# An S4D convolution and a PEER layer on one core: decays by direct exponentials, wider sine tiles, and a new order of the tables

## The chip, the cores and the metric

The kernel runs on one core of one Trainium2 chip. The metric is the device time of one execution in microseconds (us). Three executions of the kernel before took 502.75, 501.16 and 500.92 us, so its median is 501.16 us. The core has five engines with a program of their own each: TensorE (PE, with its weight loads listed as PEld), VectorE (DVE), ScalarE (ACT), GpSimd (POOL) and SyncE (SP), which issues the DMA transfers. Each runs its instructions in order, and they wait for one another by semaphores. SBUF holds 128 partitions; PSUM has eight banks of 512 fp32 words per partition, which TensorE writes and DVE and ACT read.

## The reference

Two layers on a sequence of 2048 tokens with 512 channels. The first is an S4D convolution with 128 complex states for each channel:

```python
dt = jnp.exp(log_dt)
A = -jnp.exp(log_A_real) + 1j * A_imag
C = (C_real + 1j * C_imag) * dt[:, None]
P = jnp.exp((A * dt[:, None])[:, :, None] * pos[None, None, :])
K = 2.0 * jnp.einsum("dn,dnl->dl", C, P).real
y = jnp.fft.irfft(jnp.fft.rfft(u_t, L2) * jnp.fft.rfft(K, L2)[None, :, :], L2)[:, :, :L]
return y.transpose(0, 2, 1) + u * D_skip[None, None, :]
```

It is applied to the layer norm of `x = A_u`, and `h = x + ...`. The second layer picks, for each of 32 heads, the best of 16 x 16 experts by two products with keys, and adds the expert's value times a gelu; its input is the layer norm of `h`.

## The kernel before

The work falls into a front half, the convolution, which ends about 298 us into the span, and a back half, the PEER layer. The change touches the front half alone.

The convolution of length 2048 is done as matmuls with transform matrices, in four **quarters** c of 128 channels. For each quarter there is

- `u_s1` and `k_s1`: stage 1 of the transform of the input (tile s1u) and of the kernel (s1k), four pieces kt for each. A piece is 32 matmul records with 64 columns of weights and 128 columns moved, and two copies of 128x512 by ACT out of PSUM. The input pieces `xs` are normed first, by a subtraction and a product on DVE.
- `u_s2` and `k_s2`: stage 2 (s2yu, s2yk), eight pieces for each. On the s2yk pieces DVE multiplies the two spectra (yk and U). In the last quarter, one of its three products is done on POOL (U from ki, L743), for which ACT copies ki out of PSUM.
- `k_ia`: the first inverse stage (ia), eight pieces, into T, from which ib makes the output later.

The kernel K that s1k takes is made from 32 **tables**, i = 0 to 31, eight for each quarter and 16 channels in each. A table needs the phases and the decays of 128 states at 64 short and 32 long distances, 96 columns for each channel; a state stands on each partition. `phases` (POOL, L557) adds step angles into the tile pg. `powers` (POOL, L570 to L573) builds the decays by repeated products from eleven exponentials per channel, the tile E, which ACT makes at L373; the second half of E goes to DRAM (e_d) and comes back later. `heads` (L579 to L581) multiplies the amplitudes Mg in. `mags` (L588) makes 64 columns of each channel of the tile mg by one outer product of eight heads and eight steps, and `tails` (L594) the other 32, the far distances. Then `trig` on ACT makes the sine (L647) and the cosine (L644 and L645) of the phases into PSUM tiles of one bank each, and six products on DVE (L651 to L664) form gf (sine) and mg (cosine). `kgen` (L690) multiplies each table's far and near columns into kps, and ACT and DVE take K from there.

Steps, bases, powers and heads are made for 64 channels at a time (tiles PS and TS, two buffers each); pg, mg and gf have two buffers each. All PSUM tiles of the front half are of one bank, from a pool psA of seven; psK holds the norm's mean and deviation (pc).

The order of all operations on all engines is a table of numbers, ORDER, in which the operations of the plan are emitted; an engine runs its operations in that order and never another. SP issues all loads, also in that order. The products of w_q with the keys (wps, wh, w_d) for the back half are spread through the front half, and go through DRAM.

## Time and profile before

| what | us |
|---|---|
| median of three executions | 501.16 |
| the profiled execution | 502.31 |
| its span in the profile | 500.5 |
| first s1u matmul | 71.98 |
| first ib matmul | 297.91 |
| busy in the span: PE, DVE, ACT, POOL | 448.6, 408.5, 300.2, 325.0 |

Busy time of an engine is the time in which it has at least one instruction; the chain of a profile is the sequence of work and waits that ended last, followed back from the end. A row of a group names the line, the engine, the operation, the tile written and those read, and the shape with the count; behind the bar stand the busy time in us, the mean of one in ns, and how long the engine was idle just before these instructions, and for what. A row of a stretch gives its start and end and its length in us, the busy time of the engines with the number of instructions, the clock granted to TensorE, the share of the DMA engines and GB/s. A row of the chain in order of time gives the start, the length, and what ran.

### The profile page before, as it was taken

The page shows a single profiled execution, that of the slowest core. Times are in us where ns is not written, and L with a number is a line of the kernel's source. Part 1 is how long each engine was busy: PE and PEld are TensorE (multiplying, and loading weights), DVE is VectorE, ACT ScalarE, POOL GpSimd, SP SyncE. Part 2 cuts the span into 40 slices and gives each one's busy share as a digit, 9 for nine tenths or more (in the row PEclk, how much of TensorE's full clock was granted, in tenths as well). Part 3 has the DMA queues.
Part 4 walks back from the last instruction along what each step waited for, and adds up shares of the span by engine and source line. Part 5 has one row for each costly group of instructions (what it writes and reads, how often), then busy time and mean ns, then how long its engine had stood idle before and what let it go on. Part 6 is the DMA issues. An engine that isn't in the chain of part 4 may idle for free.

```text
span 500.5 us, 16696 instructions
## 1 busy us (share of the span) xinstructions
PE 448.6 (90%) x7206; PEld 393.6 (79%) x7206; DVE 408.5 (82%) x708; ACT 300.2 (60%) x596; POOL 325.0 (65%) x344
## 2 busy tenths in 40 slices
PE   0545879999999999999999689999999999999985
PEld 0324669989999989999998688887878888787874
DVE  4879998989988998799775494878979686978994
ACT  4796789986997689966996263454043430416231
POOL 3988997999999999989864303652263516535130
PEclk9999979999999999999999899999999999999999
DMA  7916885354200740045242757320171311010012
GB/s 259 413 52 211 275 297 173 145 156 195 65 3 9 266 131 24 3 102 218 64 162 72 227 158 251 110 103 1 61 226 54 117 56 44 1 45 0 1 51 78
DMA packets 27361, 61.04 MB, mean 122 GB/s; under 512 B 7028, under 2 KB 14456, under 8 KB 26136
## 3 DMA queue, kind: packets, MB, share of 16 engines
q1 hardware_dynamic: 27288, 59.98, 35.3%
q8 instruction: 56, 0.92, 0.8%
q14 instruction: 17, 0.14, 0.1%
HBM read 46.08 MB, written 13.89 MB: 120 GB/s over the span
## 4 chain that ended last, share of the span: by engine, by line
PE 69%; DVE 19%; ACT 5%; issue 2%; DMA 2%; POOL 1%; SPq 0%; ACTq 0%; DVEq 0%
PE sc L1150 14%; PE ia L764 12%; PE s1k L471 6%; PE kps L690 6%; PE s1u L471 5%; DVE oh L1280 5%; PE s2yu L488 5%; PE xu L1157 4%; PE s2yk L488 3%; PE ib L1036 3%; PE o L1327 2%; PE wps L828 2%; PE cnt L1290 2%; DVE U L733 2%; DMA wq<-wq 2%
## 5 line engine op out<-in xcount | busy, mean ns | idle before, releaser
L588 POOL TENSOR_TENSOR mg<-TS 128x1024 f32<-128x1024 f32 x32 | 62.7, 1958 | 11.4 <-PE kps L690 11.1
L557 POOL TENSOR_TENSOR pg<-PS 128x1024 int32<-128x1024 int32 x32 | 68.8, 2152 | 1.0 <-ACT t L644 0.9
L1280 DVE TENSOR_SCALAR oh<-idxb,ec_s 128x2048 bf16<-128x2048 bf16 (+1 forms) x72 | 50.3, 756 | 6.9 <-ACT idxb L1262 6.9
L764 PE MATMUL ia<-ca_s,U 128*128 128x128 f32 x256 | 50.6, 280 | 0.8 <-POOL U L743 0.8
L1192 POOL TENSOR_TENSOR ks<-kq 128x512 f32<-128x512 bf16 x16 | 17.3, 1079 | 49.0 <-DVE kq L1186 48.4
L1060 POOL TENSOR_TENSOR vs<-hc 128x256 f32<-128x256 f32 x8 | 6.3, 789 | 59.7 <-ACT hc L1083 59.7
L645 ACT ACTIVATE t<-t,halfpi 128x512 f32<-128x512 f32 x64 | 42.4, 662 | 2.1
L1150 PE MATMUL sc<-w_hi,hhi 128*128 128x480 f32 x128 | 42.5, 413 | 0.0
L764 PEld LDWEIGHTS ia<-ca_s,U 128*128 128x128 f32 x256 | 39.8, 196 | 1.0 <-POOL U L743 1.0
L644 ACT ACTIVATE t<-pg 128x512 f32<-128x512 int32 x64 | 38.9, 607 | 0.5 <-DVE U L735 0.4
L690 PE MATMUL kps<-mg 128*32 128x64 f32 x1024 | 34.6, 233 | 5.0 <-DVE mg L660 2.8
L764 PE MATMUL ia<-ca_s,yk 128*128 128x128 f32 x192 | 38.0, 280 | 0.6 <-DVE U L735 0.3
L1150 PE MATMUL sc<-w_hi,hlo 128*128 128x480 f32 x128 | 38.4, 381 | 0.0
L1150 PE MATMUL sc<-w_lo,hhi 128*128 128x480 f32 x128 | 38.4, 380 | 0.0
L647 ACT ACTIVATE t<-pg 128x512 f32<-128x512 int32 x64 | 37.9, 608 | 0.3 <-DVE gf L655 0.2
L594 POOL TENSOR_TENSOR mg<-TS 128x512 f32<-128x512 f32 x32 | 37.4, 1172 | 0.1
L690 PE MATMUL kps<-gf 128*32 128x64 f32 x1024 | 34.4, 231 | 0.6 <-issue 0.6
L690 PEld LDWEIGHTS kps<-mg 128*32 128x32 f32 x1024 | 26.0, 117 | 9.2 <-POOL mg L594 4.7
L471 PE MATMUL s1u<-c_s,xs 128*64 128x128 f32 x512 | 33.1, 285 | 0.0
L488 PE MATMUL s2yk<-yk,c_s 128*128 128x128 f32 x256 | 32.6, 279 | 0.4 <-ACT yk L474 0.4
L488 PE MATMUL s2yu<-yu,c_s 128*128 128x128 f32 x256 | 31.9, 279 | 0.1
L471 PE MATMUL s1k<-c_s,k 128*64 128x128 f32 x512 | 31.4, 279 | 0.5 <-DVE k L702 0.5
(200 smaller groups left out, 1385.2 us busy)
## 6 DMA issues: line engine op xcount, KB each, us to landing
wq<-wq SPq DMA_DIRECT2D x25, 512.0 KB, 4.6
t_d<-T SPq DMA_DIRECT2D x24, 256.0 KB, 4.5
Tb<-t_d SPq DMA_DIRECT2D x8, 768.0 KB, 6.6
x<-xa SPq DMA_DIRECT2D x8, 512.0 KB, 6.4
xs<-xb SPq DMA_DIRECT2D x16, 256.0 KB, 3.3
xt<-xt SPq DMA_DIRECT2D x8, 512.0 KB, 4.2
out<-ob SPq DMA_DIRECT2D x7, 512.0 KB, 3.0
c_s<-wq SPq DMA_DIRECT2D x4, 512.0 KB, 10.2
```

The source lines that it names most:

```text
L471: T.matmul(ps[64 * k:64 * k + 64, g, :], lhs8(4 * n + g), c1_s[:, k], start=True, stop=True)
L488: T.matmul(ps[:, k, :], c2_s[:, kk, :], y[:, :, kk, :], start=True, stop=True)
L557: G.tensor_tensor(view(pg, 0, [[32, 2 * NC], [8, 4], [1, 8]]), view(t["PS"], 1024 + off, [[1, 2 * NC], [128, 4], [0, 8]]), view(t["PS"], 8 ...
L588: G.tensor_tensor(view(mg, 0, [[96, NC], [8, 8], [1, 8]]), view(ts, 512 + 8 * o, [[8, NC], [1, 8], [0, 8]]), view(ts, 8 * o, [[8, NC], [0, ...
L594: G.tensor_tensor(view(mg, 64, [[96, NC], [8, 4], [1, 8]]), view(ts, 1536 + o, [[1, NC], [64, 4], [0, 8]]), view(ts, 1024 + 8 * o, [[8, NC ...
L644: A.activation(p, pg[:, :, k], AF.Abs)
L645: A.activation(p, p, AF.Sin, scale=-SINSCALE, bias=halfpi)
L647: A.activation(p, pg[:, :, k], AF.Sin, scale=SINSCALE)
L690: T.matmul(kps[32 * q:32 * q + 32, 2 * g + h, :], m[:, d, 64:96], m[:, d, 0:64], start=(e == 0), stop=(e == 1))
L764: T.matmul(ps[:, g, :], t[:, 4 * n + g].rearrange("p a b -> p (a b)"), ca_s[:, s, :], start=(s == 0), stop=(s == 1))
L1150: T.matmul(ps[:, 512 * h:512 * h + 480], t[x_][:, q, ts], I[w_][:, q, 480 * h:480 * h + 480], start=(q == 0 and x_ == w_), stop=(q == 3 an ...
L1280: V.tensor_scalar(oh[:, :, 0:ln], t["idxb"][:, :, sl], S["ec"][:, 4 * e + j:4 * e + j + 1], None, op0=ALU.is_equal)
```

## The change

It consists of these parts.

1. **Decays.** The powers, the tails, the tile E and its way through DRAM go. A tile X with 48 rows for 128 channels (one buffer) holds every decay that is needed, each made by ACT as an exponential of its own from the rate `al` (kept in a tile): seven small steps, eight heads' distances, and 32 far distances (`LAGS`). The channels are handled in five units, of 64, 64, 128, 128 and 128 (`UNITS`); the exps of a unit overwrite those of the unit before. `heads` multiplies Mg into rows 9 to 15 of X. `mags` takes the eight steps and heads from X, where neighbours lie 128 words apart, and the far halves on DVE multiply the sine or cosine with rows 16 to 47 of X directly (`xf`). Steps and bases (PS, one buffer) are made for a unit.
2. **Sine tiles.** The sine and cosine of a table are one tile of two banks each, from a pool psT of two; three operations of 128x1024 on ACT take the place of six of 128x512. psA has four banks, psK is gone. Signs move from one product to another.
3. **Norm.** Subtraction and product of all 16 pieces xs run on POOL rather than DVE (`SUBS`, `MULS`).
4. **Stage 1.** A piece is done in two halves of the rows, 64x64 weights with 64 columns moved: 64 records into both banks of a psT tile, copied by one ACT operation of 128x1024.
5. **Last quarter.** Stage 2 is split into two halves of the channels; the first half's s2yk needs kt 0 and 1 only, and the ia pieces 0 to 3 need only the first four products.
6. **Order.** ORDER is made anew, with 1607 operations rather than 1729.

```diff
-    psA = ab.enter_context(tc.tile_pool(name="psA", bufs=7, space=PSUM))
-    psK = ab.enter_context(tc.tile_pool(name="psK", bufs=1, space=PSUM))
+    X = tb.tile([P, 48, 128], F32, tag="X", name="X", bufs=1)
+    PS = tb.tile([P, 3072], I32, tag="PS", name="PS", bufs=1)
+    psA = ab.enter_context(tc.tile_pool(name="psA", bufs=4, space=PSUM))
+    psT = ab.enter_context(tc.tile_pool(name="psT", bufs=2, space=PSUM))
...
+    UNITS = ((0, 64), (64, 64), (128, 128), (256, 128), (384, 128))
+    LAGS = [1.0 * k for k in range(8)] + [8.0 * k for k in range(8)] + [64.0 * k for k in range(32)]
+    ROWS = (range(1, 8), range(9, 16), range(17, 25), range(25, 33), range(33, 41), range(41, 48))
...
+            for x in ROWS[k]:
+                A.activation(X[:, x, o:o + n], al[:, a:a + n], AF.Exp, scale=-LAGS[x])
...
     def stage1(dst, lhs8, kt, nm, r, tiles, key):
...
-                for g in range(4):
+            for g in range(8):
+                for h in range(2):
+                    rows = slice(64 * h, 64 * h + 64)
                     for k in range(2):
-                        T.matmul(ps[64 * k:64 * k + 64, g, :], lhs8(4 * n + g), c1_s[:, k], start=True, stop=True)
+                        T.matmul(ps[h][64 * k:64 * k + 64, g, :], lhs8(g)[rows], c1_s[rows, k], start=True, stop=True)
...
-        plan.add("DVE", 0.60, sub, r=["mu"], w=[xs_k], t=[xs_k])
-        plan.add("DVE", 0.60, mul, r=["rs"], w=[xs_k], t=[xs_k])
+        plan.add(*("POOL", 1.15) if SUBS[n] else ("DVE", 0.60), lambda: norm(G if SUBS[n] else V, ALU.subtract), r=["mu"], w=[xs_k], t=[xs_k])
+        plan.add(*("POOL", 1.15) if MULS[n] else ("DVE", 0.60), lambda: norm(G if MULS[n] else V, ALU.mult), r=["rs"], w=[xs_k], t=[xs_k])
...
-    def powers(i):
...
+    def heads(a, w):
+        o = a % 128
+        G.tensor_copy(X[:, 8, o:o + w], Mg[:, a:a + w])
+        G.tensor_tensor(X[:, 9:16, o:o + w], X[:, 9:16, o:o + w], Mg[:, a:a + w].unsqueeze(1).to_broadcast([P, 7, w]), op=ALU.mult)
...
     def mags(i):
...
         G.tensor_tensor(view(mg, 0, [[96, NC], [8, 8], [1, 8]]),
-                        view(ts, 512 + 8 * o, [[8, NC], [1, 8], [0, 8]]),
-                        view(ts, 8 * o, [[8, NC], [0, 8], [1, 8]]), op=ALU.mult)
-
-    def tails(i):
...
+                        view(X, 1024 + o, [[1, NC], [128, 8], [0, 8]]),
+                        view(X, o, [[1, NC], [0, 8], [128, 8]]), op=ALU.mult)
...
+        def far(cos):
+            V.tensor_mul((t["mg"] if cos else gf_())[:, :, f_], xf, wide(cos)[:, :, up])
...
-            job, k = stage2(c, "yk", k4, deps + u_k + [("U", c, k4)], tiles)
+            h = c > 2 and k4 < 4
+            job, k = stage2(c, "yk", k4, (deps[0:4] if h else deps) + (u_k[0:4] if h else u_k) + [("U", c, k4)], tiles)
```

What this does to the order on the engines is shown at three places. A row has the line, the operation, the tile written, those read, and the shape; x2 counts equal instructions in a row. First POOL, at the start of table 16 and its unit. Before, while the tables run on (here the last rows of one group of 64 channels, the heads of the next into TS, and the first two tables of it):

```order
L588 TENSOR_TENSOR mg_2087<-TS_1367 128x16x64
L579 COPY TS_1874<-Mg 128x64
L580 TENSOR_TENSOR TS_1874<-Mg,E_1810 128x64
L581 TENSOR_TENSOR TS_1874<-TS_1874,E_1810 128x128
L594 TENSOR_TENSOR mg_2087<-TS_1367 128x16x32
L557 TENSOR_TENSOR pg_2111<-PS_1565 128x1024
L588 TENSOR_TENSOR mg_2158<-TS_1874 128x16x64
L557 TENSOR_TENSOR pg_2185<-PS_1565 128x1024
L594 TENSOR_TENSOR mg_2158<-TS_1874 128x16x32
L588 TENSOR_TENSOR mg_2253<-TS_1874 128x16x64
L594 TENSOR_TENSOR mg_2253<-TS_1874 128x16x32
```

Now, from the last mags of table 15 to the phases of table 16:

```order
L587 TENSOR_TENSOR mg_2311<-X 128x16x64
L526 TENSOR_TENSOR xs_3_2307<-xs_3_2307,nrm 128x512 x2
L580 COPY X<-Mg 128x128
L581 TENSOR_TENSOR X<-X,Mg 128x896
L526 TENSOR_TENSOR xs_2_2176<-xs_2_2176,nrm 128x512
L555 COPY PS<-RS_78 128x256
L556 TENSOR_TENSOR PS<-RS_78 128x256
L558 TENSOR_TENSOR PS<-PS 128x256x2
L558 TENSOR_TENSOR PS<-PS 128x256x4
L565 COPY PS<-A_79 128x256
L567 TENSOR_TENSOR PS<-PS 128x256 x3
L587 TENSOR_TENSOR mg_2669<-X 128x16x64
```

The tails have gone, the norm stands among the rows, and the heads (L580, L581) come behind the last mags of the unit before, with the steps of the new unit behind them.

Second ACT, at the same place of the program. Now, from the cosine of table 15 (t_15) on:

```order
L631 ACTIVATE t_15_2320<-pg_2309 128x1024
L633 ACTIVATE t_15_2320<-t_15_2320,halfpi 128x1024
L434 ACT_TABLE_LOAD
L434 ACTIVATE X<-al 128x128 x7
L487 COPY yk_2417<-s1k_2_2377 128x1024
L487 COPY yk_2417<-s1k_0_2419 128x1024
L695 COPY k_3_2485<-kps_3_2335 128x512
L770 COPY T_1854<-ia_2_2368 128x128x4
L487 COPY yk_2417<-s1k_1_2488 128x1024
L487 COPY yk_2417<-s1k_3_2523 128x1024
L434 ACTIVATE X<-al 128x128 x15
```

The piece before shows two tables in a row as they then stood on ACT (tables 22 and 23, with the copies among them):

```order
L645 ACTIVATE t_22_2954<-t_22_2954,halfpi 128x512
L698 COPY k_2_2957<-kps_2_2864 128x512
L474 COPY yu_2974<-s1u_0_0_2897 128x512
L644 ACTIVATE t_22_2998<-pg_2948 128x512
L645 ACTIVATE t_22_2998<-t_22_2998,halfpi 128x512
L474 COPY yu_2974<-s1u_0_1_2906 128x512
L647 ACTIVATE t_23_3013<-pg_3005 128x512
L772 COPY T_2797<-ia_6_2976 128x128x4
```

Exponentials and a table load now stand between the cosine of one unit and the sine of the next, with the copies of stage 1 among them.

Third PE, at the end of the last quarter, from the last kps on. Before:

```order
L690 MATMUL kps_3_3972<-gf_3937 32x64 x4
L471 MATMUL s1k_2_0_4041<-c_s,k_2_3898 64x128 x8
L471 MATMUL s1k_3_1_4052<-c_s,k_3_4039 64x128 x8
L471 MATMUL s1k_3_0_4063<-c_s,k_3_4039 64x128 x8
L836 MATMUL wpt_4073<-ident,wt_3373 128x128
L488 MATMUL s2yk_0_4076<-yk_3914,c_s 128x128 x4
L488 MATMUL s2yk_1_4085<-yk_3914,c_s 128x128 x4
```

Now:

```order
L687 MATMUL kps_3_4278<-gf_4313 32x64 x4
L484 MATMUL s1k_2_4428<-c_s,k_2_4260 64x64 x32
L504 MATMUL s2yk_1_4461<-yk_4357,c_s 128x64 x8
L504 MATMUL s2yk_0_4477<-yk_4357,c_s 128x64 x8
L484 MATMUL s1k_3_4487<-c_s,k_3_4426 64x64 x32
L504 MATMUL s2yk_2_4528<-yk_4357,c_s 128x64 x8
L504 MATMUL s2yk_3_4545<-yk_4357,c_s 128x64 x8
L504 MATMUL s2yk_4_4587<-yk_4357,c_s 128x64 x8
```

Stage 1 of kt 3 now stands between pieces of stage 2, whose first two need kt 0 and 1 only, and the pieces of w_q (L836, L828) no longer stand among the pieces of s2yk.

More of the change, by code (lines that the diff above doesn't have):

```diff
@@ L625, in factors @@
[L625 removed]
+        u = 0 if i < 4 else i // 8 + 1
+        a, w = UNITS[u]
+        p, c = int(i > 3), w > 64
+        first = 16 * i == a
+        if first:
+            if u > 1:
+                for k in range(6):
+                    decay(u, k)
+                plan.group = f"tab{i}"
+            plan.add("POOL", 4.2 if c else 2.46, lambda: steps(a, w), r=[("RS", p)], w=[("PS", u)], t=[f"PS{u}"], lag=0)
+            plan.add("POOL", 2.95 if c else 2.04, lambda: bases(a, w), r=[("A0", p)], w=[("PS", u)], t=[f"PS{u}"], lag=0)
@@ new lines, in cosine @@
+        def cosine():
+            mg, p = t["mg"], wide(1)[:, :, lo]
+            V.tensor_mul(mg[:, :, up], mg[:, :, up], p)
+            V.tensor_mul(mg[:, :, lo], mg[:, :, lo], rev(1))
+        def far(cos):
+            V.tensor_mul((t["mg"] if cos else gf_())[:, :, f_], xf, wide(cos)[:, :, up])
+        xk = [f"XF{u}"] + ["XF01"] * (u < 2)
+        xr = [("X", u, k) for k in range(2, 6)]
+        a = plan.add("ACT", 0.93, lambda: trig(0), r=[("pg", i)], lag=0.2, t=tiles, take="psT", tab="trig")
@@ new lines, in tables @@
+        a = plan.add("DVE", 1.2, sine, r=[("mg", i)], w=[("tab", i, 0)], t=tiles, after=[a])
+        plan.add("DVE", 0.6, lambda: far(0), r=xr, w=[("tab", i, 1)], t=tiles + xk, give="psT", after=[a])
+        a = plan.add("ACT", 0.94, lambda: trig(1, 1), r=[("pg", i)], lag=0.2, t=tiles, take="psT")
+        a = plan.add("ACT", 0.95, lambda: trig(1, 2), t=tiles, tab="trig", after=[a])
+        a = plan.add("DVE", 1.2, cosine, r=[("mg", i), ("tab", i, 0)], w=[("tab", i, 2)], t=tiles, after=[a])
@@ L674, in kgen @@
+        plan.add("DVE", 0.6, lambda: far(1), r=xr, w=[("tab", i, 3)], t=tiles + xk, give="psT", after=[a])
     def kgen(i):
```

292 lines of the change are left out of this document (130 added, 162 removed), and 157 rows, old and new, of the table ORDER.

## The prediction

> **What bounds the kernel now.** I read the page's totals and its chain first, then the stretches of the span, then the chain in order of time.
>
> ```profile
> PE 448.6 (90%) x7206; PEld 393.6 (79%) x7206; DVE 408.5 (82%) x708; ACT 300.2 (60%) x596; POOL 325.0 (65%) x344
> PE 69%; DVE 19%; ACT 5%; issue 2%; DMA 2%; POOL 1%; SPq 0%; ACTq 0%; DVEq 0%
> ```
>
> TensorE holds 69% of the chain, but those are averages over unlike stages. The back half (from ib) keeps its instructions and their order, so only the part ahead of it can move. Busy time by stretch (PE, PEld, DVE, ACT, POOL, each with its instruction count):
>
> ```profile
> 0.00:72.00 72.00, 36.38 (x684) 26.13 (x686) 58.89 (x164) 51.12 (x132) 59.49 (x73) 0.98 0.72 254
> 72.00:150.00 78.00, 77.12 (x1500) 72.78 (x1504) 70.65 (x117) 68.00 (x131) 72.06 (x65) 0.98 0.37 125
> 150.00:207.00 57.00, 56.64 (x1098) 53.08 (x1090) 50.60 (x83) 46.97 (x91) 55.82 (x53) 1.00 0.29 95
> 207.00:262.50 55.50, 55.46 (x1125) 52.10 (x1114) 47.38 (x77) 45.97 (x89) 46.07 (x39) 1.00 0.36 122
> 262.50:298.00 35.50, 29.45 (x300) 27.50 (x299) 21.72 (x40) 18.17 (x38) 10.10 (x8) 0.95 0.52 162
> 298.00:500.50 202.50, 193.51 (x2544) 162.02 (x2544) 159.23 (x230) 70.03 (x118) 81.51 (x109) 1.00 0.22 74
> ```
>
> In the middle quarter (150 to 207) PE works 56.64 of 57.00 us and POOL 55.82; DVE and ACT have 6 and 10 us to spare. Two engines are full at once, so relief of PE alone would bring one microsecond. The chain in order of time gives the marks that I use:
>
> ```profile
> 89.57 1.10 PE kps L690 x64
> 92.66 1.90 PE s1k L471 x32
> 260.57 1.98 PE kps L690 x128
> 262.55 3.09 PE s1k L471 x48
> 266.30 1.17 PE s2yk L488 x8
> 278.98 1.27 POOL U L743
> 280.29 15.90 PE ia L764 x126
> 297.91 1.99 PE ib L1036 x128
> ```
>
> The kps matmuls of table 7 end at 90.7 and those of table 31 at 262.5: a ramp of 90.7, then three quarters of (262.5 - 90.7)/3 = 57.3 us, then a tail of 297.9 - 262.5 = 35.4 us until ib. I forecast these three terms. The profiled execution took 502.31 us (span 500.5, 1.8 beside it), 1.15 above the median 501.16; I sum against the execution and carry the difference to the median.
>
> **The change part by part, per quarter (eight tables).**
>
> PE, stage 1. Now 32 records of 128 columns take 1.90 us per kt (92.66). Afterwards there are 64 records of 64 columns, in four quadrants. The kps row has 64 records of 64 columns, four abreast, in 1.10. If quadrants run as freely, a kt saves 0.8 and a quarter's eight kt save 6.4: PE 56.6 - 6.4 = 50.2. If only two run abreast, the 64 half-length records take the same 1.90 and nothing is saved. I take 0.8, because its row has the same count and width.
>
> ```profile
> L557 POOL TENSOR_TENSOR pg<-PS 128x1024 int32<-128x1024 int32 x32 | 68.8, 2152 | 1.0 <-ACT t L644 0.9
> L588 POOL TENSOR_TENSOR mg<-TS 128x1024 f32<-128x1024 f32 x32 | 62.7, 1958 | 11.4 <-PE kps L690 11.1
> L594 POOL TENSOR_TENSOR mg<-TS 128x512 f32<-128x512 f32 x32 | 37.4, 1172 | 0.1
> L573 POOL TENSOR_TENSOR TS<-TS,E 128x768 f32<-128x768 f32 x8 | 12.6, 1579 | 0.6
> L573 POOL TENSOR_TENSOR TS<-TS,E 128x384 f32<-128x384 f32 x8 | 7.5, 938 | 0.6
> L571 POOL COPY TS<-E 128x192 f32<-128x192 f32 x8 | 4.6, 572 | 0.0
> L570 POOL MEMSET TS<- 128x192 f32 x8 | 3.6, 456 | 0.0
> L541 POOL TENSOR_TENSOR PS<-PS 128x512 int32<-128x512 int32 x8 | 8.3, 1039 | 0.6
> L541 POOL TENSOR_TENSOR PS<-PS 128x256 int32<-128x256 int32 x8 | 4.9, 614 | 0.6
> L550 POOL TENSOR_TENSOR PS<-PS 128x128 int32<-128x128 int32 x24 | 12.5, 519 | 1.9
> L581 POOL TENSOR_TENSOR TS<-TS,E 128x128 f32<-128x128 f32 x8 | 3.7, 459 | 0.6
> ```
>
> POOL. Out go the tails, 8 x 1.172 = 9.4, and the powers, 2 x (1.579 + 0.938 + 0.572 + 0.456) = 7.1. Steps and bases run on 128 channels at once, which halves eight instructions' fixed cost: L541 grows by 425 ns for 256 elements, so 614 - 425 = 189 ns is fixed, 8 x 0.19 = 1.5 saved. The old and new heads, small copies and products, I leave equal. In comes the norm: eight products of 512 at 1.04 to 1.17 (L541, L594), say 1.10: 8.8. The mags now read one operand in steps of 512 bytes. The only strided read of before is L550 (one operand in steps of 32 bytes, 519 ns). The same width without a stride is 459 (L581), or 614 - 212 = 402 by L541's slope: 60 to 117 ns for 128 elements, so 0.48 to 0.94 us for 1024. A stride of 512 bytes isn't in the trace, so nothing (0) and more than 0.94 are possible too. I take 0.70, the middle of the two comparisons: 8 x 0.70 = 5.6. Sum: 55.8 - 9.4 - 7.1 - 1.5 + 8.8 + 5.6 = 52.2, and 46.6 without the stride.
>
> [...]
>
> ```profile
> L644 ACT ACTIVATE t<-pg 128x512 f32<-128x512 int32 x64 | 38.9, 607 | 0.5 <-DVE U L735 0.4
> L645 ACT ACTIVATE t<-t,halfpi 128x512 f32<-128x512 f32 x64 | 42.4, 662 | 2.1
> L647 ACT ACTIVATE t<-pg 128x512 f32<-128x512 int32 x64 | 37.9, 608 | 0.3 <-DVE gf L655 0.2
> L474 ACT COPY yu<-s1u 128x512 f32<-128x512 f32 x32 | 18.5, 592 | 5.8 <-PE s1u L471 5.5
> L373 ACT ACTIVATE e<-pb 128x256 f32<-128x256 f32 x11 | 3.5, 404 | 0.0
> L373 ACT ACTIVATE E<-pb 128x192 f32<-128x192 f32 x11 | 2.9, 349 | 0.3 <-DVE pb L359 0.3
> L394 ACT ACT_TABLE_LOAD x2 | 2.6, 1283 | 0.8 <-PEq L1437 0.7
> ```
>
> ACT. In come 45 exps of 128 columns. The e row shows eleven in 3.5 us of busy time, 0.32 each, and 64 columns cost 404 - 349 = 55 ns; 128 columns fewer give 0.21, say 0.20: 9.0. Two table loads at 1.283 add 2.6, since exp and sine take turns once per unit. Trig goes from 2 x (0.607 + 0.662 + 0.608) = 3.75 to three of double width; 64 columns at 55 ns make 512 more cost 0.44, so 1.05 + 1.10 + 1.05 = 3.20, 8 x 0.55 = 4.4 saved. Stage 1's sixteen copies of 0.592 become eight of 1.03: 1.2 saved. ACT: 47.0 + 9.0 + 2.6 - 4.4 - 1.2 = 53.0.
>
> ```profile
> L505 DVE TENSOR_TENSOR xs<-xs,pc 128x512 f32<-128x512 f32 x16 | 10.8, 681 | 0.7 <-ACT pc L260 0.7
> L508 DVE TENSOR_TENSOR xs<-xs,pc 128x512 f32<-128x512 f32 x16 | 10.9, 684 | 0.3
> L655 DVE TENSOR_TENSOR gf<-mg,t 128x512 f32<-128x512 f32 x32 | 21.8, 682 | 3.0 <-POOL mg L594 2.0 <-ACT t L647 0.9
> L1199 DVE TENSOR_SCALAR ei<-ks 128x64 int32<-128x64 int32 x16 | 4.3, 268 | 1.9 <-POOL ks L1194 1.9
> L309 DVE TENSOR_SCALAR pa<-par 128x64 f32<-128x64 f32 x3 | 0.7, 224 | 0.1
> ```
>
> DVE. The norm leaves: 4 x (0.681 + 0.684) = 5.5. The far halves (L655 and its cosine twin) read X in steps of 512 bytes. A 64-wide operation whose input steps (L1199) takes 268 ns, the contiguous one (L309) 224: 44/64 x 512 = 0.35 us more, 16 x 0.35 = 5.6. DVE stays at 50.7; without the price it is 45.1.
>
> **What the quarter makes of it.** Four engines stand at 50.2, 52.2, 53.0 and 50.7. If all overlapped, a quarter would take 53, 4 less than now. They can't: X has one buffer. The exps of the next unit wait for the last mags and far halves, and ACT's order puts 45 exps (9.0), two loads (2.6) and some fourteen copies (seven of stage 1 at 1.03, the rest shorter, about 10) between table 15's cosine and table 16's sine: some 22 us without trig. Eight tables then take 8 x (2.15 + 2.66) = 38.5 on POOL. Without overlap that is 60. In the gap PE has stage 1 and 2 and DVE the products, so the gap isn't empty; but at table 15 the heads wait on POOL for 14 exps with steps, bases and a norm product queued behind them, and the first mags after those. Between 53 and 60 I go somewhat by the serial end and take 57.3: **no gain per quarter**.
>
> **Ramp.** By the same prices POOL loses powers and tails and gets as much back in the first norm and the strides; ACT has 90 exps of 64 columns for the 33 wider ones. I take 0, between -5 (no stride) and +4 (ACT late). The x loads stand earlier on SP, which brings s1u forward, but table 7 waits for POOL and ACT, not for s1u.
>
> **Tail.** Now: s2yk starts 3.8 us after table 31's kps (266.30), DVE's eight products follow, and the last U on POOL starts 12.7 us behind s2yk's start (278.98), 1.58 per product. ia waits for that U, starts 17.8 after the kps (280.29) and runs 15.9. Afterwards one kt with two halves of s2yk follow the kps, four products feed the first ia, and the other four run beside ia. By the same rows: s2yk at +1 to +2, four products at 1.58 to about +8.5, U 1.27, a wait for ACT's evictions in between, so ia from about +11 for 15.9 us and, as now, ib 1.7 behind its end (296.2 to 297.9): +28.4. 35.4 - 28.4 = **-7.0**. If the later products gate ia, half of it is lost.
>
> Sum: 0 + 0 - 7.0 gives 495.3 for an execution like the profiled one, **494.2 on the median**. Differences under 0.5% (2.5 us) can't be told from no change.
>
> **Rivals.**
> - *Full overlap or strides for nothing* (0.19). For it: three engines stand below 53. Against: one X buffer and orders that cannot bend. Quarters of 53: 3 x -4.3 = -13, with the tail 481.
> [...]
> - *Quadrants not abreast* (0.05), the change not doing what it says: PE stays at 56.6, and about 3 us of each switch add to it: 502 to 503.
> - *Two sine slots shared with stage 1* (0.24, slower). A table holds one slot for sine (1.05 + 2 x 0.68 + 1.03, with waits about 3.6) and one for cosine (2.15 + 2.39, about 4.6): 8.2 of two slots per 4.8 us, 85% taken, and stage 1 takes 2.4 more wherever it stands between tables; seven banks served this before. PE is in order, so a stage 1 that waits for a slot holds up kps, and kps frees mg for POOL. It decides once a table takes over 5.0 us on its longest engine; at 5.6 it costs 0.8 x 24 = 19, less some 5 that the quarters' waits would hide: 494 + 14 = 508.
>
> **The numbers.** The forecast gets 0.36, from 488 to 498. Faster 0.36 + 0.19 = 0.55, same 0.16 + 0.05 = 0.21, slower 0.24. The range 481 to 510 takes in the lower end of the first rival and most of the last.
>
> **What would show it.** Right: s1 rows of 64 in about 1.0 us, mags near 2.66, far halves near 1.03, kps of table 7 near 91 and of table 31 near 262, ib 28 us later. [...]

## The result and the profile after

The changed kernel is slower: 530.64 us (median of four executions, 529.91 to 531.22) against 501.48 us (four, 500.92 to 502.75). The ratio is 1.0575, with an interval of 1.055 to 1.06. The profiled execution took 529.91 us, its span 527.5. Executions of some variants below lie 10 to 20 us apart, which their profiles tie in part to a stretch at half clock in the last quarter (last section), so ratios are formed from their shorter executions (for `e14_whole_contig` from all).

The page's totals and its chain of waits after:

```profile
PE 449.7 (85%) x8358; PEld 388.8 (74%) x8358; DVE 411.4 (78%) x677; ACT 326.3 (62%) x667; POOL 327.8 (62%) x276
PE 46%; DVE 24%; POOL 14%; ACT 6%; issue 6%; DMA 2%; SPq 0%; POOLq 0%; ACTq 0%; DVEq 0%
```

PE works 1.1 us more than before, DVE and POOL 2.9 and 2.8, and ACT, which had most to spare, 26. Yet PE's share of the chain falls from 69% to 46%, and DVE and POOL take it over. No engine has become the bound by its total; what has changed is how they lie beside one another.

The stretches between the marks of the prediction (end of kps of tables 7, 15, 23, 31, first ib):

```profile
0.00:92.20 92.20, 56.40 (x1338) 41.44 (x1338) 73.00 (x179) 73.00 (x200) 67.57 (x63) 0.94 0.74 254
92.20:158.10 65.90, 55.66 (x1459) 50.26 (x1456) 52.18 (x76) 59.34 (x117) 63.57 (x39) 1.00 0.25 78
158.10:223.10 65.00, 52.87 (x1210) 48.16 (x1212) 52.24 (x76) 53.77 (x105) 53.14 (x32) 0.95 0.20 67
223.10:290.90 67.80, 59.23 (x1430) 55.74 (x1434) 52.27 (x76) 53.61 (x97) 50.55 (x27) 0.97 0.20 75
290.90:322.30 31.40, 31.36 (x387) 30.89 (x389) 21.42 (x36) 15.86 (x29) 10.98 (x8) 1.00 0.47 154
```

| term | before | after | change |
|---|---|---|---|
| ramp, to table 7 | 90.7 | 92.2 | +1.5 |
| three quarters, table 7 to 31 | 171.9 | 198.7 | +26.8 |
| tail, table 31 to first ib | 34.4 | 31.4 | -3.0 |
| from ib to the end | 203.5 | 205.2 | +1.7 |

The first ib record of before stands at 297.0 here, 0.9 ahead of the one on its chain that the prediction used. The loss is in the quarters. In the third row all four engines work 52 to 54 us of 65; before, PE worked 56.64 of 57.00. In the second row POOL is nearly full, 63.57 of 65.90, since ten of the norm's 32 operations lie there, and only five and three in the next two. The clock explains little: by the rows, 5% of 65.0 us and 3% of 67.8 us were lost to it, some 5 us of the 26.8 at most.

The time between one table's kps and the next shows the new shape. Before, tables 16 to 23 ended 5.5, 6.4, 14.8, 5.9, 8.8, 2.9, 8.4 and 4.7 us apart, with the other work between them. After, the first of them comes 30.3 us behind table 15 (28.5 and 31.9 us in the other quarters), and then seven come about 5 us apart. I call the long one the **hole**. Busy time of hole and tables by turns, three quarters (start and end and length, then PE, PEld, DVE, ACT, POOL):

```profile
92.20:119.60 27.40, 25.32 (x575) 23.17 (x573) 21.17 (x31) 25.54 (x69) 26.77 (x21) 1.00 0.34 107
119.60:158.10 38.50, 30.34 (x887) 27.09 (x886) 31.01 (x45) 33.79 (x49) 36.81 (x19) 1.00 0.18 57
158.10:187.30 29.20, 23.36 (x488) 21.06 (x487) 21.28 (x32) 23.22 (x62) 20.18 (x15) 1.00 0.43 146
187.30:223.10 35.80, 29.51 (x726) 27.10 (x730) 30.96 (x45) 30.55 (x44) 32.96 (x17) 0.90 0.01 3
223.10:253.90 30.80, 27.83 (x629) 26.19 (x630) 20.82 (x31) 24.49 (x62) 23.66 (x16) 1.00 0.21 80
253.90:290.90 37.00, 31.41 (x805) 29.55 (x808) 31.45 (x46) 29.12 (x36) 26.89 (x11) 0.95 0.19 70
```

Among the tables POOL is nearly full in the first two quarters (36.81 of 38.50, 32.96 of 35.80), by phases of 2.15 and mags of 2.75 us; in the third no engine is (31.45 of 37.00 at most). In the first hole PE, ACT and POOL are nearly full as well, and DVE has 21 of 27; in the other two no engine works more than 23.36 of 29.20 and 27.83 of 30.80 us. The two stretches follow one another and add up.

The chain of waits in the second hole, in order of time:

```profile
158.13 1.68 PE s1k L484 x99
159.81 1.40 issue
161.22 0.71 PE s1k L484 x29
161.95 1.02 ACT yk L487
163.01 1.17 PE s2yk L508 x8
164.28 0.70 DVE yk L730
165.00 0.69 DVE U L731
165.70 0.69 DVE U L733
...
182.02 0.69 DVE U L733
182.75 0.69 DVE gf L650
183.95 1.03 DVE gf L659
187.27 1.10 PE kps L687 x64
```

The last pieces of stage 1 come behind table 15's kps, then stage 2, then 24 products on DVE from 164.3 to 182.7 with one pause of 1.3 us, and only then table 16's first product. ACT in the same hole, from its timeline:

```profile
152.07 1.28 ACT L434 ACT_TABLE_LOAD   x1
153.36 1.51 ACT L434 ACTIVATE X<-al 128x128 f32<-128x128 f32 x7
...
161.95 1.01 ACT L487 COPY yk<-s1k 128x1024 f32<-128x1024 f32 x1 [1.65 <-PE s1k L484]
162.86 3.10 ACT L434 ACTIVATE X<-al 128x128 f32<-128x128 f32 x15
...
177.29 1.28 ACT L635 ACT_TABLE_LOAD   x1
178.58 1.03 ACT L635 ACTIVATE t<-pg 128x1024 f32<-128x1024 int32 x1
```

From the end of table 15's cosine to table 16's sine there are 26.5 us, 22.5 of them work (ACT's four waits for PE's pieces and kps add up to 3.9):

```profile
152.05:178.58 26.53, 22.14 (x628) 20.07 (x627) 15.67 (x25) 22.49 (x63) 21.82 (x17) 1.00 0.36 125
```

At the other two switches, from table 7 to 8 and from 23 to 24, the same gap is 23.7 us, with 22.3 and 21.7 us of ACT's work.

The groups of the front half whose durations the prediction set (busy us, mean ns, idle us before them):

```profile
L587 POOL TENSOR_TENSOR mg<-X 128x1024 f32<-128x1024 f32 x32 | 87.9, 2747 | 21.0 <-PE kps L687 13.7 <-DVE gf L651 4.8 <-ACT X L434 2.3
L574 POOL TENSOR_TENSOR pg<-PS 128x1024 int32<-128x1024 int32 x32 | 68.6, 2148 | 0.2
L526 POOL TENSOR_TENSOR xs<-xs,nrm 128x512 f32<-128x512 f32 x32 | 40.6, 1282 | 3.9 <-PE s2yu L508 2.6 <-DMA xs<-xb 0.6
L633 ACT ACTIVATE t<-t,halfpi 128x1024 f32<-128x1024 f32 x32 | 34.8, 1089 | 0.8
L659 DVE TENSOR_TENSOR gf<-X,t 128x512 f32<-128x512 f32 x32 | 33.5, 1047 | 0.0
L631 ACT ACTIVATE t<-pg 128x1024 f32<-128x1024 int32 x32 | 32.9, 1029 | 6.5 <-DVE mg L659 5.1 <-DVE k L699 0.5 <-DVE gf L659 0.5
L434 ACT ACT_TABLE_LOAD x5 | 6.4, 1283 | 0.1
```

### The profile page after: what moved, and what is told of

The parts are those of the page before. It is cut to its first block, busy times and chain, and to the rows that moved or that the text cites. A ratio compares the mean times of both kernels' runs of the same rounds, so it can differ in the third digit from the quotient of the medians.

```text
span 527.5 us, 19002 instructions
## 1 busy us (share of the span) xinstructions
PE 449.7 (85%) x8358; PEld 388.8 (74%) x8358; DVE 411.4 (78%) x677; ACT 326.3 (62%) x667; POOL 327.8 (62%) x276
## 3 DMA queue, kind: packets, MB, share of 16 engines
q1 hardware_dynamic: 27000, 57.03, 31.8%
q8 instruction: 65, 1.06, 0.8%
## 4 chain that ended last, share of the span: by engine, by line
PE 46%; DVE 24%; POOL 14%; ACT 6%; issue 6%; DMA 2%; SPq 0%; POOLq 0%; ACTq 0%; DVEq 0%
PE sc L1148 12%; POOL mg L587 5%; PE ia L762 5%; DVE oh L1278 4%; PE xu L1155 4%; PE kps L687 3%; POOL xs L526 3%; PE s2yk L504 3%; PE s2yu L504 2%; PE s1k L484 2%; DVE mg L659 2%; PE o L1325 2%; PE s2yk L508 2%; POOL pg L574 2%; PE cnt L1288 2%
## 5 line engine op out<-in xcount | busy, mean ns | idle before, releaser
L587 POOL TENSOR_TENSOR mg<-X 128x1024 f32<-128x1024 f32 x32 | 87.9, 2747 | 21.0 <-PE kps L687 13.7
L574 POOL TENSOR_TENSOR pg<-PS 128x1024 int32<-128x1024 int32 x32 | 68.6, 2148 | 0.2
L762 PE MATMUL ia<-ca_s,yk 128*128 128x128 f32 x192 | 40.4, 293 | 3.4 <-ACT wh L838 1.2
L526 POOL TENSOR_TENSOR xs<-xs,nrm 128x512 f32<-128x512 f32 x32 | 40.6, 1282 | 3.9 <-PE s2yu L508 2.6
L434 ACT ACTIVATE X<-al 128x128 f32<-128x128 f32 (+1 forms) x225 | 42.7, 282 | 0.1
L631 ACT ACTIVATE t<-pg 128x1024 f32<-128x1024 int32 x32 | 32.9, 1029 | 6.5 <-DVE mg L659 5.1
L635 ACT ACTIVATE t<-pg 128x1024 f32<-128x1024 int32 x32 | 33.1, 1033 | 4.0 <-DVE gf L659 2.4
L633 ACT ACTIVATE t<-t,halfpi 128x1024 f32<-128x1024 f32 x32 | 34.8, 1089 | 0.8
L762 PEld LDWEIGHTS ia<-ca_s,yk 128*128 128x128 f32 x192 | 30.6, 200 | 5.6 <-ACT wh L838 1.4
L659 DVE TENSOR_TENSOR gf<-X,t 128x512 f32<-128x512 f32 x32 | 33.5, 1047 | 0.0
L650 DVE TENSOR_TENSOR gf<-mg,t 128x512 f32<-128x512 f32 x32 | 21.9, 684 | 14.5 <-POOL mg L587 7.6
```

Source lines behind the costliest of these rows:

```text
L434: A.activation(X[:, x, o:o + n], al[:, a:a + n], AF.Exp, scale=-LAGS[x])
L526: eng.tensor_tensor(d["xs"], d["xs"], nrm[:, k].unsqueeze(1).to_broadcast([P, 8, 64]), op=op)
L574: G.tensor_tensor(view(pg, 0, [[32, 2 * NC], [8, 4], [1, 8]]), view(PS, 2048 + off, [[1, 2 * NC], [256, 4], [0, 8]]), view(PS, 8 * off, [[ ...
L587: G.tensor_tensor(view(mg, 0, [[96, NC], [8, 8], [1, 8]]), view(X, 1024 + o, [[1, NC], [128, 8], [0, 8]]), view(X, o, [[1, NC], [0, 8], [1 ...
L631: A.activation(p, pg, AF.Abs)
L633: A.activation(p, p, AF.Sin, scale=-SINSCALE, bias=halfpi)
```

## The experiments

The theories, with the letters of the expectations: A, the chain of stage 1, stage 2 and DVE's products sets the hole. B, ACT's exponentials set it. C, the strided reads of X do. D, the norm on POOL does. E, the quadrants of stage 1 are pure gain. F and G, they are worth little, or 8 to 12 us, in the changed kernel. J, exponentials and products are two chains abreast, N, with stage 2 of the input three. L, what the quadrants lose is the clock of a PE that is too little busy, M, it is not. P, the channel halves cost what their doubled pieces cost. "Before" took 501 to 503 us in the median beside every run.

**Exponentials left out** (`e1_no_exps`).

```diff
-            for x in ROWS[k]:
+            for x in ROWS[k] if u < 2 else ():
```

> The changed kernel with the exps of the units 2, 3 and 4 left out (their table loads go with them; the later units use the decays of the first two, so the output is another), order unchanged. Theory A, the phases stand in series by order: between the last kps of a quarter and the first of the next DVE's 24 spectrum products (18.5 us) stand ahead of the next table, and the exps only fill the same hole beside them; then the hole shrinks by 1 to 4 us at each of three switches, 3 to 12 us in all, to about 520 to 527. Theory B, the exps and their two table loads (9.4 + 2.6 us) hold the hole: 10 to 12 us at each switch, 30 to 36 in all, to about 495 to 500.

Measured: 524.36 and 535.75 us. In the profile of the longer one the holes are 27.6, 30.5 and 40.9 us, the third with the clock halved. Nine microseconds of ACT's work per hole are gone and the first two holes stay (28.5 and 30.3 with them), so B falls. The second gap between cosine and sine stays as well, although ACT works half as long in it; some 2 us of it are clock that is lost here:

```profile
152.54:177.96 25.42, 21.80 (x618) 20.13 (x617) 15.38 (x24) 11.24 (x18) 21.34 (x17) 0.93 0.38 137
```

The exponentials thus didn't hold the gap. The shorter execution lies within A's 520 to 527.

**Contiguous reads** (`e2_contig`, and `e12_contig_again` with more executions). X is laid out by channel, so the mags' and far halves' neighbours lie side by side.

```diff
-    X = tb.tile([P, 48, 128], F32, tag="X", name="X", bufs=1)
+    Xn = tb.tile([P, 128, 48], F32, tag="X", name="X", bufs=1)
+    X = Xn.rearrange("p n x -> p x n")
...
-                        view(X, 1024 + o, [[1, NC], [128, 8], [0, 8]]),
-                        view(X, o, [[1, NC], [0, 8], [128, 8]]), op=ALU.mult)
+                        view(Xn, 8 + 48 * o, [[48, NC], [1, 8], [0, 8]]),
+                        view(Xn, 48 * o, [[48, NC], [0, 8], [1, 8]]), op=ALU.mult)
```

> The changed kernel with X laid out channel by channel (48 words together), so that mags and far halves read in steps of 4 bytes; the exps and heads write in steps of 192 bytes instead. Theory C, the strided reads are a large part of the loss: mags fall from 2.75 to about 1.95 us and far halves from 1.04 to 0.68, a table's pace on POOL from 4.9 to 4.1, 0.8 x 24 = 19 us less after the ramp and 3 to 6 in it, about 507. If theory A holds as well, the pace counts in full as the tables run alone, so the same number; the holes between quarters stay at 27 to 31 us. If another engine sets the pace (DVE's six products, or a slot of the sine tiles) it falls by less than 0.4 a table, under 10 us, over 520. A price for ACT's strided writes would show as exps over 0.21 us.

> The same kernel as the first run with X laid out channel by channel, for more executions. By the tables' spacing in that run's first two quarters (4.2 to 4.5 us rather than 4.8 to 5.0) seven spacings a quarter give 3 to 4 us, ten in all: 518 to 522. If the strides cost nothing: 530.

Measured: 525.71 and 546.04 us, and with more executions 527.67 in the median (521.56 to 529.63), ratio 1.046 (1.039 to 1.053). The mags fall back to before's duration; the group of `e2_contig`:

```profile
L588 POOL TENSOR_TENSOR mg<-X 128x1024 f32<-128x1024 f32 x32 | 62.5, 1952 | 38.5 <-PE kps L688 29.7 <-DVE gf L652 4.0 <-ACT t L632 2.6
```

Some 25 us of POOL's busy time go, and about 17 us of the idle time in front of the mags come in their place. In `e12_contig_again` the tables then follow at 4.3 to 4.7 us rather than 5, and the first two holes stay near 30 (29.8 and 30.5). The strides are worth 3 us in the median here and 9 at most (with the last quarter's halves undone 9 in the median, see `e14_whole_contig`). That is far from C's 507, and of the second run only the shortest execution lies in the 518 to 522 that were expected. C falls as the main cause.

**Norm on DVE** (`e3_norm_dve`).

```diff
-    SUBS, MULS = ([int(x) for x in y] for y in ("1111111111111111", "1111111111111111"))
+    SUBS, MULS = ([int(x) for x in y] for y in ("0000000000000000", "0000000000000000"))
```

> The changed kernel with the norm back on DVE (subtraction and product of all sixteen pieces), order unchanged. Theory A: DVE is the engine in both phases, 32 x 0.6 = 19 us more work for it, of which what stands at the switches (about 20 of the 32) delays the products: 0 to 12 us slower. Theory D, the norm on POOL (1.28 each, 41 us in all) holds the heads and the mags: 8 to 20 us faster.

Measured: 570.76 us, ratio 1.137 (1.134 to 1.140), worse than any guess. Its groups:

```profile
L526 DVE TENSOR_TENSOR xs<-xs,nrm 128x512 f32<-128x512 f32 x32 | 38.7, 1223 | 0.3
L484 PE MATMUL s1u<-c_s,xs 64*64 64x64 f32 x1024 | 22.4, 244 | 15.4 <-DVE xs L526 14.5 <-issue 0.9
```

On DVE one of them takes 1.22 us in the mean, 0.68 before, and 32 stand in places of the order that were made for POOL, where stage 1 waits for them. The holes become 40.4, 31.8 and 48 us. It says that this order has no room on DVE. D's gain of 8 to 20 us did not come, but the run doesn't show what POOL's norm costs, since its new place costs more than it could free.

**Quadrants alone, in the kernel before** (`e4_quad_before`): stage 1 in two halves of the rows, copies as before in two parts, ORDER unchanged.

```diff
-                    for k in range(2):
-                        T.matmul(ps[64 * k:64 * k + 64, g, :], lhs8(4 * n + g), c1_s[:, k], start=True, stop=True)
+                    for h in range(2):
+                        rows = slice(64 * h, 64 * h + 64)
+                        for k in range(2):
+                            T.matmul(both[h][64 * k:64 * k + 64, g, :], lhs8(g)[rows], c1_s[rows, k], start=True, stop=True)
```

> The kernel before with only stage 1 changed: 64x64 quadrants in two banks of psA, two copies by ACT as before. The prediction's reading (PE and POOL both full, so relief of PE alone brings about a microsecond a quarter): stage 1 falls from 1.90 to 1.16 us a kt, and the whole from 501 by 0 to 4 us. Theory E, PE alone bounded the front half (69% of the chain): 6 us a quarter, 18 to 24 in all, about 480.

Measured: 518.85 us (516.69 and 521.01), ratio 1.034 (1.023 to 1.044): 17 us slower. E falls, and so does my reading of nearly no change. Two of its quarters:

```profile
158.50:217.80 59.30, 50.72 (x1354) 47.35 (x1358) 50.46 (x82) 47.36 (x91) 55.70 (x53) 1.00 0.26 91
217.80:277.10 59.30, 51.70 (x1347) 47.43 (x1347) 46.63 (x75) 45.90 (x88) 44.45 (x37) 1.00 0.33 118
```

PE is relieved of about 6 and 3 us a quarter (57.04 of 57.40 and 54.86 of 54.90 before), and the quarters take 2 and 4 us longer. PE's busy time shrank, at the full clock, and the quarters grew.

**The same with PE filled up** (`e10_quad_filled`): six matmuls of 128 columns ahead of each piece, whose results are overwritten. They were meant to keep PE as busy as in the kernel before.

```diff
+                    for g in range(6):
+                        T.matmul(both[g % 2][0:64].rearrange("p a b -> p (a b)")[:, 0:128], lhs8(g), ...)
```

> The kernel before with quadrants in stage 1, as in the earlier run (518.9), and in each piece six matmuls of the old form ahead of them, whose result is overwritten: PE is busy 1.9 us a piece as before. Theory L, the loss of that run is the clock, which falls to half when PE pauses: without the pauses back to 500 to 507, with less than 8 us of lost clock ahead of ib (15.4 there, 5.1 before). Theory M, the loss is the number of instructions (instruction supply) or the banks: 515 to 525.

Measured: 538.36 us (536.07 to 539.14), ratio 1.068 (1.064 to 1.072). The filling is too much: the six come to 12 records and 1.52 us, so that a piece takes 2.6 us rather than 1.9, and PE's busy time rises from 434.1 to 472.0 us, 23 above the kernel before. In a quarter PE is then nearly full (61.51 of 63.10 us from 168.5 to 231.6), which lengthens the quarters by itself. The clock lost ahead of ib (the length of each 2 us times one less the granted clock) goes from 15.4 to 10.2 us, not below the 8 that L asked for. The run thus decides neither L nor M. Pauses of PE and half clock go together only in part: in the kernel before the granted clock fell to 0.50 at 68.6 and at 280.2 us, in pauses of 1.19 and 0.85 us, for 6.8 and 3.4 us (the 5.1 us lost ahead of ib there), and it stood at 1.00 from 30 to 36 us, where PE worked 0.83 us.

**Old stage 1 in the changed kernel** (`e7_s1_old`): 32 records of 128 columns into the same two banks.

```diff
-            for g in range(8):
-                for h in range(2):
-                    rows = slice(64 * h, 64 * h + 64)
-                    for k in range(2):
-                        T.matmul(ps[h][64 * k:64 * k + 64, g, :], lhs8(g)[rows], c1_s[rows, k], start=True, stop=True)
+            for g in range(8):
+                for k in range(2):
+                    T.matmul(ps[64 * k:64 * k + 64, g, :], lhs8(g), c1_s[:, k], start=True, stop=True)
```

> The changed kernel with stage 1 in its old form (32 records of 128 columns with all rows, 1.9 us a kt), into the same two-bank tiles with the same copies and the same order. Theory F, relief of PE buys nothing here since PE waits anyway, and its pauses cost half clock and instruction supply: within -6 and +4 us of 530. Rival G, stage 1 stands on the series path between the quarters (two to three kt of eight) and in the ramp: 0.75 us x 10 to 16 = 8 to 12 us slower, about 540.

Measured: three executions of 533.89 to 535.04 us, two longer; ratio 1.065 (1.060 to 1.069). Here the quadrants gain some 4 us of the 24 that they take off PE. G falls; F's bound of 534 is met within 1 us.

**Another order** (`e5_order`, and `e6_contig_order` with contiguous X). ORDER is replaced by another legal one that was meant to shorten the holes.

> The changed kernel with another ORDER and nothing else: the spectrum products of a quarter are spread among the next quarter's tables where they can be, and the first exps of a unit come before stage 1 of the last kernel pieces. Theory A, the order puts the products and the tables in series: a quarter then takes what its fullest engine has, POOL with 8 x (2.15 + 2.75) + 8 x 1.28 + about 9.5 for steps, bases and heads = 59 us rather than 66, three quarters give back 15 to 21, about 510 to 515. Rival H, the one buffer of X makes the series and no order can help: 525 to 531.

> The kernel with X channel by channel (contiguous reads) with an ORDER of its own, made in the same manner as for the other. Theory A and C together: POOL falls to 8 x (2.15 + 1.95) + 10.2 + 9.5 = 52.5 a quarter, DVE to 46, ACT stays near 53; quarters of 55 to 57, three times 10 less than 66, about 498 to 503. If the strides don't bind once the order is mended: the same as the run before, 510 to 515. Rival H: over 515.

Measured: 576.19 (564.69 to 583.07) and 546.17 us (544.57 to 559.61). Both miss, and neither tests A as was meant: the new orders kept holes of 28 to 33 us, and table 7 came at 102.6 and 101.3 us. More of the loss lies behind the first ib, where the same 2558 records of PE took 230.7 and 222.8 us at a granted clock of 0.93 and 0.95, rather than 205.2 at 1.00. The three quarters themselves took 211.9 and 187.1 us, 198.7 in the changed kernel, so the second of the orders does gain 11.6 us there. All that follows is that a rebuilt order costs tens of microseconds as easily as it gains any.

**Products cut to an eighth** (`e8_short_prod`), in quarters 0 to 2, so that DVE has 10 instead of 21 us of work in a hole.

```diff
+                if c < 3:
+                    pv, uv, kv = pv[:, 0:4], uv[:, 0:4], kv[:, 0:4]
                 V.tensor_mul(kv, pv, uv)
```

> The changed kernel with DVE's spectrum products of the quarters 0 to 2 cut to an eighth of their columns (the rest of the spectra stays unmultiplied, so the output is another), order unchanged. They take some 5 us instead of 17 in each of three holes between the quarters. Theory A, the products in series make the hole: 10 to 12 us less per hole, about 495 to 500. Theory J, two chains of nearly the same length stand side by side in the hole, DVE's products and ACT's exps with the next sine, each hiding the other: 1 to 4 us per hole, 519 to 527. Theory K, neither (PE's pauses, instruction supply): 527 to 533.

Measured: 524.40 us (523.70 to 525.90), ratio 1.042 (1.038 to 1.046). The hole that the chain above gave to DVE, without its products:

```profile
155.60:181.70 26.10, 22.51 (x482) 20.76 (x482) 10.09 (x32) 22.98 (x62) 20.93 (x15) 1.00 0.46 161
```

It loses 3 us, and then ACT and PE are the fullest in it. Its chain of waits no longer runs over the products but over PE: s1k, s2yk, s1u and s2yu. A falls as the single cause.

**Products and exponentials** (`e9_short_no_exps`), both edits.

> Both cuts at once: products cut to an eighth and the exps of the units 2 to 4 left out. Theory J: only now the hole shrinks, from 28 to 30 us to about 16 to 18, 10 to 13 us at each of three, about 492 to 502; that is far more than the two cuts give alone when added. Theory A: the same as the short products alone. Theory K: over 515.

Measured: 532.13 us in the median, 522.44 the shortest. J falls: with the products gone, taking out the exponentials brings nothing more. In the second hole PE remains, by the same chain from s1k over s2yk, s1u to s2yu:

```profile
155.90:182.10 26.20, 22.54 (x486) 20.82 (x487) 10.13 (x32) 14.61 (x23) 19.84 (x14) 1.00 0.46 162
```

**Three chains** (`e11_three_cut`): as well as these, the matmuls of s2yu leave in quarters 1 to 3.

```diff
             y = Q[c][nm]
+            if skip:
+                return
```

> The kernel with short products and without the exps of the later units, and besides without stage 2 of the input (s2yu) in the quarters 1 to 3; ACT's copies into U read yu instead. Theory N, the order puts three chains side by side in the hole between two quarters, ACT's exps, DVE's products and PE's stages 1 and 2, each of them about as long as the hole, so that one or two can go and nothing is won; with PE's chain shortened too by 8 x 1.0 us (8 x 1.86 in the last quarter) the hole falls from 27 to 17 to 20 us, and the time by 20 to 30 us from the fast runs of the two cuts (522), about 492 to 503. If the hole stays over 25 us, something else holds it (POOL's steps and heads, or the first table's own path), and the time is over 512.

Measured: 518.84 us (515.67 to 520.62), ratio 1.032 (1.028 to 1.037). N's 492 to 503 falls too. Its holes:

```profile
91.40:116.70 25.30, 21.76 (x542) 19.55 (x539) 10.00 (x31) 14.07 (x22) 24.67 (x21) 1.00 0.36 116
156.60:178.80 22.20, 17.05 (x435) 15.42 (x435) 10.04 (x32) 14.41 (x24) 19.92 (x14) 1.00 0.55 192
213.00:238.50 25.50, 17.54 (x562) 15.96 (x566) 10.15 (x32) 15.24 (x21) 23.56 (x16) 0.95 0.25 95
```

In the first hole POOL is now nearly full (24.67 of 25.30), and the chain of waits runs over it alone: the norm, the steps, the bases and the heads of the next unit. In the second the chain still runs over PE's remaining pieces (s1k, s2yk, s1u), and no engine is full. No run took POOL's work out by itself.

**Channel halves undone** (`e13_whole`; `e14_whole_contig` with contiguous X): stage 2 of the last quarter in one piece again, ORDER mended at 22 places so that it stays legal.

```diff
-            h = c > 2 and k4 < 4
+            h = False
```

> The changed kernel with the last quarter's stage 2 in whole pieces as before (128 columns; what needs all of stage 1 is put behind it in ORDER, 22 places). Theory P, the split costs: sixteen pieces of 1.86 us become 0.98, 7 us of PE in the third hole and 7 in the tail, of which the tail gives back 3 to 4 as its early start goes; 4 to 10 us faster, 521 to 527, and no execution with a long stretch of half clock ahead of the last tables. Rival: the split is hidden by the products and exps in the hole and pays in the tail: 530 to 535.

> The same with X channel by channel. Theory P and the strides: the contiguous kernel (527.7 median, 521.6 its fastest) loses its half-clock stretches and the 64-column pieces: 508 to 517. Rival: half clock comes at that place whatever runs there: 520 to 530.

Measured: 531.35 us (530.76 to 532.59), no change, so the rival holds; and 522.57 (514.74 to 526.13), ratio 1.042 (1.038 to 1.046), by its median in the rival's range; of its six executions the shortest lies in P's (514.74), the next between the two (518.96). In the profile of `e13_whole` the last of the three quarters takes 65.2 us rather than 67.8, and the tail 35.9 rather than 31.4, some 3 to 4 us of it by a clock of 0.90: what the whole pieces save in the quarter is lost in the tail. `e14_whole_contig` is the best of the changed kernels that compute everything; its median lies 4% behind the kernel before, its shortest execution 2.6%. Against `e13_whole` the contiguous reads gain 9 us in the median and 16 between the shortest executions, more than in the pair above; the holes stay at 29 to 30 us.

**Channel halves alone, in the kernel before** (`e15_halves_before`).

> The kernel before with only the last quarter's stage 2 in channel halves (its order as it is, so the early start isn't used). Theory P: PE is full in that quarter, 8 x 0.88 = 7 us later at the last kps, and the tail 2 to 7 later as eight pieces of 1.86 outlast the products: 509 to 516. Rival: hidden, 501 to 505.

Measured: 512.46 us (511.55 to 513.23), ratio 1.021 (1.019 to 1.023). P holds: table 31 comes 6.8 us later (269.4) and the tail, 38.2, is 3.8 longer. In that order the halves bring nothing, they only cost.

No version beat the kernel before.

## Why the prediction was wrong

**The prices were about right.** Mags took 2.75 us (2.66 was said), far halves 1.04 to 1.05 (1.03), sine and cosine 1.03, 1.03 and 1.09 (1.05, 1.05, 1.10), a stage 1 piece 1.16 (1.10). The norm was short at 1.28 (1.10), 5.8 us in all. For PE, POOL, ACT and DVE 50.2, 52.2, 53.0 and 50.7 us in a quarter were forecast; 52.9, 53.1, 53.8 and 52.2 were measured in the middle one. That agreement is in part luck: the middle quarter holds only five of the norm's operations and none of the heads. The means of the three quarters are 55.9, 55.8, 55.6 and 52.2, up to 6 us above the forecast.

**The step that failed is "What the quarter makes of it".** It had a gap of ACT without trig, 22 us by ACT's own work, and 38.5 us of POOL for eight tables, serial 60; then it took 57.3, since the gap "isn't empty". The quarters took 65.9, 65.0 and 67.8. Two things were wrong in it.

The credit for overlap, some 3 us, had no row behind it and did not come; the quarters took more than the 60 of both terms in series. The gaps were 23.7, 26.5 and 23.7 us, and what is left of each quarter is 42.2, 38.5 and 44.1. That the middle one equals the forecast's 38.5 is chance. POOL did make two mags and two phases of the new unit within the second gap, 9.8 us, but then waited 2.6 and 4.8 us, for PE's s2yu and for a product of DVE (gf, L651), before the third mag.

And the gap was read as ACT's work, while work of other engines sets it. ACT's work in it came to 22.5 us, as I had it, but without half of it (`e1_no_exps`) the gap hardly shrank. PE's stages and DVE's products, which I let run inside the gap, stand in series there: stage 1 behind the last kps, then stage 2, then 24 products of 0.7 us, all ahead of the next table's first product on DVE. In the second hole `e8_short_prod`, `e9_short_no_exps` and `e11_three_cut` show what is under the products: 29.2 us with them, 26.1 and 26.2 by PE's chain without them, 22.2 with that chain shortened as well. In the first hole POOL's chain is about as long (25.3 of 27.4 us were left). Engine totals of 50 to 56 us in a quarter say nothing of this; before, that work lay between the tables.

**The ramp** was right: +1.5, in a range of -5 to +4.

**The tail** had the right sign and less than half of the size, -3.0 rather than -7.0. I let ia start 11 us behind the last kps, on half of the pieces (11, 15.9 and 1.7 add up to 28.6, not 28.4). The chain of waits there:

```profile
288.99 1.86 PE kps L687 x64
...
292.32 3.72 PE s2yk L504 x32
296.03 1.09 PE s1k L484 x64
297.12 10.86 PE s2yk L504 x96
307.99 9.00 PE ia L762 x80
```

All eight pieces of s2yk stand ahead of ia in PE's order, which the rows quoted ahead of the prediction began to show, and each takes 3.72 / 2 = 1.86 us, for half-width records are twice as many and no shorter (0.116 us each; 24 of the full width take 2.94 us, 0.122 each). Together 14.6 us, and ia starts 17.1 behind kps, as before (17.7). I never priced part 5's doubled pieces, here or in the last quarter, where stage 2 of the input is doubled too.

**The rivals.** Full overlap is out. Quadrants are abreast (64 records in 1.16 us, 32 of the old kind in 1.90). The 0.16 among the chances for "same" stands for mags at half as much again, a price that no run shows: they took 40% more than before, 2.747 us for 1.958, and `e2_contig` returns 1.952, so the stride is the cause. That is 0.09 us above my estimate of 2.66, 2.8 us for all 32 mags, which would not have given 530. The slot rival's 508 had the right side and the wrong place: ACT is idle ahead of L631, which takes a slot, for 6.5 us in the whole front half, as the row above shows, and ahead of L635, the other that takes one, for 4.0, not 19.

**What stays open.** Why the quadrants alone cost 17 us in the old order: the clock explains up to 10 (15.4 us lost ahead of ib, 5.1 before), but the two quarters shown are at the full clock and lose 6 together. PE waits there for instructions to issue, and for DVE's products ahead of s1k and s1u (8.3 and 8.4 us of idle time before these in the whole kernel, by the releasers 1.3 of it issue and 13.5 DVE; 0.5 and 0.0 before), and I could not part the two; the run with PE filled up filled it too much to tell. Quadrants cost 17 and halves 11 in the old order, but undoing them in the new one cost 4 and changed nothing, so these numbers don't add up to the 29 us. No run shows the decays or the new ORDER alone. A second buffer for X, which would let the exponentials of a unit run among the tables of the one before, was not tried, nor was it shown that some order without holes exists with one.

## What to carry to other kernels

Here a buffer that is filled in one piece for eight tables, in an order made for it, came with a pipeline of two stretches that add up; which of the two makes them was not shown. In such a plan, price the longest chain of waits in each stretch, across engines, not each engine's total, and give no credit for overlap that no row shows. Even the sum of the fullest engines of the two stretches is too low (63.6, 56.3 and 59.3 us here, 65.9, 65.0 and 67.8 measured). When several chains are of nearly equal length in a stretch, removing one of them moved it by 3 us where 10 were expected, so an experiment with one cut can't clear it. A split into half-width matmuls has to be priced by records: with full-size weights, half the columns took about the same time here (0.116 us a record for 0.122).

## What the runs showed of the hardware

- **Long stretches at half clock with PE fully busy.** In one execution of `e12_contig_again` the chain and the stretches read

```profile
235.12 15.12 PE s2yu L505 x80
236.00:250.20 14.20, 14.20 (x76) 14.20 (x75) 5.85 (x10) 4.05 (x6) 2.14 (x1) 0.56 0.00 1
```

  The same 80 records take 9.14 us in the changed kernel's profile. They have full-size weights and 64 columns each, and PE is busy in all of the 14.20 us of the second row. `e1_no_exps`, `e2_contig`, `e7_s1_old` and `e9_short_no_exps` show it as well (15.1 to 15.9 us), and the longer execution of `e2_contig` has a second one in the tail, which takes 47.6 us there rather than 31.4:

```profile
295.00:325.50 30.50, 30.50 (x199) 30.26 (x199) 12.39 (x17) 8.19 (x12) 8.77 (x7) 0.50 0.22 79
```

  The profiles of `e13_whole` and `e14_whole_contig`, where these matmuls have 128 columns, don't. The first stretch costs 6 us in these 80 records alone, and such stretches explain part of the 10 to 20 us between executions of one kernel. Busy records did not bring the full clock back soon: in `e12_contig_again` the granted clock is 0.50 in each 2 us from 238 to 258, with PE busy throughout, and in `e2_contig` in all of the 30.50 us of the last row.
- **Quadrants double stage 1's records** (2048 for 1024; with the last quarter's halves 8358 for 7206 in the whole kernel), and in the second hole the chain has 1.40 us of issue in the middle of one stage 1 piece. In the groups of the whole kernel, 2.4 us of idle time before s1k and 2.4 before s1u are put down to issue, none before.
- **A table load cost its 1.283 us and no more**: the next exponential starts at 153.36, 0.01 behind its end.
- **The norm's subtractions and products on DVE took 1.22 us in the mean** in `e3_norm_dve`, against 0.68 before; most still took 0.68 or 0.69, and some up to 3.23. What lengthens the others was not tried.
